# Attention scores in two six-bank units per half, where there were three four-bank units

## The chip, the cores and the metric

The kernel runs on one core of a Trainium2 chip. The metric is the device time of one execution in microseconds, lower is better. A core has five engines that run their own instruction streams and wait for each other by semaphores: TensorE (PE, with its weight loads as PEld), VectorE (DVE), ScalarE (ACT), GpSimd (POOL) and SyncE (SP). Matmul results land in PSUM, which has eight banks of 512 fp32 columns by 128 partitions.

## The reference, cut to what matters

```python
scores = scale * q @ k.T                     # 4 batches, 8 heads, 768 positions, head size 64
keep = (key < 8) | (0 <= query - key < 96)   # 8 global keys and a local window
scores = where(keep, scores - slope[h] * dist, -1e9)
a = softmax(scores); attn = a @ v
x = attn, heads side by side                 # 3072 tokens x 512
out = (relu(x @ w_gate) * (x @ w_val)) @ w_out   # 512 -> 1536 -> 512
```

Inputs and output are fp32. The kernel computes in bf16 and fp16 with fp32 accumulation.

## The kernel before, in words

**Tiling.** The work is cut into eight halves `s` = 0 to 7: half a sequence (384 queries) of one batch. A half with even `s` is a first half of its sequence, one with odd `s` a second half. For each half the kernel computes attention of eight heads, then the feed-forward part (FFN) of its 384 tokens. While the FFN of half `c` runs on TensorE, the attention of half `c + 1` is woven in between. The change is in the attention of `s` = 2 to 7 (the third to the eighth half); the first two go another way, which the change leaves alone.

**Attention of one half.** Heads come in pairs `p` = 0 to 3, a head of a pair is `e` = 0 or 1 and lies on rows 64·e to 64·e + 63 of the array. Two pairs make a double pair `pp`. Keys come in tiles `j`; a bank group `g` = 0, 1, 2 says which key tiles share one PSUM bank. For a fixed (`pp`, `g`, `e`) one bank holds the transposed scores of two heads. The steps are:

- `score_unit` (matmul at L512): it takes one bank for each (`pp`, `g`, `e`) of its unit and fills them. These matmuls use half of the array's rows, and the two of `e` = 0 and `e` = 1 stand one after the other, so that they can run side by side.
- `unit_exp` (L521): exp of one bank on ScalarE into a buffer `es` in SBUF. It gives back a function `mask`, which multiplies `es` by the precomputed mask and bias on VectorE (L533), one instruction per key tile of the bank.
- `piece_av` (L431): for one head, `es` times values and ones into a bank of `av_ps`, four matmuls in an even half and five in an odd one, in the order of the key tiles; then log of the sums on ScalarE (L440), and after the second head of a pair the reciprocal (L445).
- `piece_norm` (L450): two VectorE multiplications, from `av_ps` to `xT`, the FFN's input. They free the two `av_ps` banks.

In a list of pieces, X is one exp with, after it, the masks of the exp before it; X(unit) puts the score matmuls ahead of it. AV(p) is two pieces, one a head, and each first emits what masks are left (`flush`). N(p) is the normalisation, and `wait` is an empty slot.

**FFN of one half.** `gate(fc)` and `val(fc)` for `fc` = 0 to 11: four matmuls each (L745) into a bank of `ff_ps`; relu of the gate on ScalarE (L754); product with the value bank on VectorE into `ht` (L761). From `fc` = 7 on, one sum of `ht` tiles a step follows the product (L624 to L627, for `c` of 2 and more). Then the second product (L631) with pieces named "1", "2", "4", "6", "5", "7", "3", results added up on VectorE (L644), and stored.

**PSUM.** Three pools share the eight banks: `qk_ps` three, `av_ps` two, `ff_ps` three. A unit takes its banks from them.

**Order.** Everything is emitted in an order written out by hand. `weave` takes the FFN pieces, each with weight 0.65, and emits an attention piece whenever the emitted weight reaches its place; `spread` puts the n pieces of a half at equal distances over 85 or 87 per cent of it (for `s` = 2 between 2 and 86 per cent of its stretch). Each engine runs its instructions in the order of emission.

Of the kernel before, what the change touches and what calls it, by code (L numbers as in the profile page):

```python
# [8 lines left out]
FP32 = mybir.dt.float32  # L9
# [7 lines left out]
def kernel(  # L17
# [12 lines left out]
    nc = tc.nc  # L30
# [10 lines left out]
    NN = 3  # L41
# [45 lines left out]
    kT = [[const.tile([128, NT, 128], BF16, name=f"kT{i}_{p}") for p in range(HP)] for i in range(2)]  # L87
# [163 lines left out]
    QKB, FFB, AVB = (qk_psum, "qk_ps"), (ff_psum, "ff_ps"), (av_psum, "av_ps")  # L251
# [168 lines left out]
    def piece_av(s, p, e):  # L420
        b, half = divmod(s, 2)
        h = 2 * p + e
        vb = vbuf[b % 2]
        av = av_psum.tile([128, 512], FP32, name="av_ps")
        av_of[s, p, e] = av
        av3 = av[:, 0:QH].rearrange("d (n p) -> d n p", n=NN)
        todo = [t for bank in banks_of_half[half] for t in bank]
        for i, (j, a, w, m) in enumerate(todo):
            es, c = es_of[s, p, j, e]
            z0 = 2 * D * h + (D if e == 0 else 0)  # L430
            nc.tensor.matmul(av3[:, :, a : a + w],  # L431
                             lhsT=vb[:, j, z0 : z0 + 128],
                             rhs=es[:, c : c + NN * w].rearrange("k (n p) -> k n p", n=NN),
                             start=(i == 0), stop=(i == len(todo) - 1),
                             skip_group_check=True)
        o0, d0 = (0, 64) if e == 0 else (64, 0)
        if e == 0:
            av_of[s, p, "l"] = rc_pool.tile([128, QH], FP32, name="lnd")
        ln = av_of[s, p, "l"]
        nc.scalar.activation(ln[o0 : o0 + 64], av[d0 : d0 + 64, 0:QH], AF.Ln, bias=0.0, scale=1.0)  # L440
        if e == 1:
            if s not in xT_of:
                xT_of[s] = xt_pool.tile([128, N_DC, QH], BF16, name="xT")
            rc = rc_pool.tile([128, QH], FP32, name="rcp")
            nc.scalar.activation(rc, ln, AF.Exp, bias=0.0, scale=-1.0)  # L445
            av_of[s, p, "r"] = rc

    def piece_norm(s, p, e):
        r = slice(64 * e, 64 * e + 64)
        nc.vector.tensor_tensor(xT_of[s][r, p, :], av_of[s, p, e][r, 0:QH], av_of[s, p, "r"][r],  # L450
                                op=ALU.mult)

    def piece_av_wide(s, p, *pools):

        b, half = divmod(s, 2)
        todo = [t for bank in banks_of_half[half] for t in bank]
        pools = pools or (AVB,)
        av = [pool.tile([128, 512], FP32, name=name) for pool, name in (pools[0], pools[-1])]
        for what in range(2):
            av3 = av[what][:, 0:QH].rearrange("d (n p) -> d n p", n=NN)  # L460
            for i, (j, a, w, m) in enumerate(todo):
                for e in range(2):
                    es, ce = es_of[s, p, j, e]
                    z0 = D + 2 * D * (2 * p + e)
                    nc.tensor.matmul(av3[64 * e : 64 * e + 64, :, a : a + w],  # L465
                                     lhsT=ones if what == 0 else vbuf[b % 2][:, j, z0 : z0 + D],
                                     rhs=es[:, ce : ce + NN * w].rearrange("k (n p) -> k n p", n=NN),
                                     start=(i == 0), stop=(i == len(todo) - 1),
                                     skip_group_check=True)
        av_of[s, p] = av  # L470

    def piece_norm_wide(s, p):
        piece_sums_wide(s, p)
        piece_mul_wide(s, p)
# [17 lines left out]
            xT_of[s] = xt_pool.tile([128, N_DC, QH], BF16, name="xT")  # L492
        nc.vector.tensor_tensor(xT_of[s][:, p, :], av_of[s, p][1][:, 0:QH], av_of[s, p, "r"], op=ALU.mult)

    def score_unit(s, groups, pools):


        b, half = divmod(s, 2)
        out = []
        for pp, g in groups:  # L500
            banks = []
            for e in range(2):
                pool, name = pools.pop(0)
                banks.append(pool.tile([128, 512], FP32, name=name))
                out.append((pp, g, e, banks[e]))
            c = 0
            for j, a, w, m in banks_of_half[half][g]:
                for p in (2 * pp, 2 * pp + 1):
                    for e in range(2):
                        r = slice(64 * e, 64 * e + 64)  # L510
                        q3 = qT2[s % 2][r, p].rearrange("d (n p) -> d n p", n=NN)
                        nc.tensor.matmul(banks[e][:, c : c + NN * w], lhsT=kT[b % 2][p][r, j, :],  # L512
                                         rhs=q3[:, :, a : a + w], start=True, stop=True)
                    c += NN * w
        return out

    def unit_exp(s, pp, g, e, ps):
        bank = banks_of_half[s % 2][g]
        cols = sum(2 * NN * w for _, _, w, _ in bank)
        es = es_pool.tile([128, 480], BF16, name="es")  # L520
        nc.scalar.activation(es[:, 0:cols], ps[:, 0:cols], AF.Exp, bias=0.0, scale=scale)  # L521

        def mask():
            c = 0
            for j, a, w, m in bank:
                n_ = 2 * NN * w
                e4 = es[:, c : c + n_].rearrange("k (i n p) -> k i n p", i=2, n=NN)
                h0 = 4 * pp + e
                mk = m_all[:, h0 : h0 + 3 : 2, 0 if j == 0 else 1, :, m : m + w]
                if w == WQ:  # L530
                    e4 = e4.rearrange("k i n p -> k i (n p)")
                    mk = mk.rearrange("k i n p -> k i (n p)")
                nc.vector.tensor_mul(e4, e4, mk)  # L533
                for i in range(2):
                    es_of[s, 2 * pp + i, j, e] = (es, c + i * NN * w)
                c += n_

        return mask

    def attention_pieces(s):  # L540
        masks, units = [], []

        def flush():
            for f in masks:
                f()
            masks.clear()

        def scores(groups, pools):
            units.extend(score_unit(s, groups, list(pools)))

        def x(scored=None):
            ready = masks[:]
            masks.clear()
            if scored:
                scores(*scored)
            masks.append(unit_exp(s, *units.pop(0)))
            for f in ready:
                f()

        U = [([(0, 0), (0, 1)], (AVB, QKB, QKB, QKB)),  # L560
             ([(0, 2), (1, 0)], (AVB, QKB, QKB, QKB)),
             ([(1, 1), (1, 2)], (AVB, QKB, QKB, QKB))]
        X = lambda u=None: [(0.0, lambda: x(u))]
        AV = lambda p: [(0.0, lambda e=e: (flush(), piece_av(s, p, e))) for e in range(2)]
        N = lambda p: [(0.0, lambda: (piece_norm(s, p, 0), piece_norm(s, p, 1)))]
        wait = [(0.0, lambda: None)]
        a0, a1 = AV(0), AV(1)

        return (X(U[0]) + X() + X() + X() + wait + X(U[1]) + X() + X() + a0[0:1] + X() + a0[1:2] + N(0) + wait
                + X(U[2]) + X() + a1[0:1] + X() + X() + a1[1:2] + N(1) + wait * 2 + AV(2) + N(2) + wait * 2  # L570
                + AV(3) + N(3))


    out_v = out.rearrange("(s p n) d -> s n p d", p=128, n=NN)

# [261 lines left out]
    def AV(s, p, *pools):  # L837
        piece_av_wide(s, p, *pools)
        piece_norm_wide(s, p)
# [139 lines left out]
    def T2_piece(p):  # L979
# [10 lines left out]
    sums_wo = [(0.0, f) for i in (0, 3) for f in weight_sums(i, i + 3)]  # L990
    weave(f1_0[G[2]] + f1_1[G[2]] + f2_0 + f2_1,
          spread(attention_pieces(2), 0.02, 0.86), spread(early_pieces(3), 0.1, 0.76),
          spread(sums_wo, 0.08, 0.4))

    for c in range(2, NHALF):
        placed = []
        if c + 1 < NHALF:
            placed.append(spread(attention_pieces(c + 1), 0.0, 0.85 if c % 2 else 0.87))
        if c + 2 < NHALF:
            load_qk(c + 2, 0, H)  # L1000
            load_v_half(c + 2)
            placed.append(spread(early_pieces(c + 2), 0.25, 0.75))
        f1, f2 = ffn_pieces(c)
        weave(f1 + f2, *placed)
# [35 lines left out]
```

The softmax here doesn't subtract the row's maximum and nothing guards it: scores larger than these inputs give would overflow.

## Time and profile before

| what | value |
|---|---|
| median of 3 runs | 237.72 us (236.86 to 237.77) |
| span of the profiled execution | 236.1 us |
| PE busy | 228.7 us, 97% |
| DVE busy | 186.9 us, 79% |
| ACT busy | 146.2 us, 62% |
| POOL busy | 89.0 us, 38% |
| score matmuls, L512 | 216, in 18 units of 8, 12 or 16 |
| attention times values, L431 | 216 matmuls, 21.4 us |
| masks, L533 | 108 instructions, 29.9 us |

An engine's busy time is the sum of its instructions' times as recorded. Matmuls overlap in the pipeline, so that TensorE's pace is read from the distance of starts rather than from durations. The granted TensorE clock is full over nearly all of the span.

### The profile page before, as it was taken

The numbers are of one execution on the slowest core, as the hardware profiler recorded it, in microseconds if no ns is written. First come the engines' busy times: TensorE is split into PE (matmuls) and PEld (weight loads), VectorE is DVE, ScalarE is ACT, GpSimd is POOL, SyncE is SP. The second block draws the span as 40 slices with busy tenths as digits, with TensorE's granted clock in tenths as the row PEclk, the third lists the DMA queues.
The fourth block names the chain that finished last, engine by engine and source line by source line (L and its number), as shares of the span: only waits on it lengthen the run. The fifth ranks groups of instructions, "written<-read, shape, count | busy, mean of one in ns | idle before, by whom it ended". The sixth has DMA issues, their size and how long they took to land.

```text
span 236.1 us, 5512 instructions
## 1 busy us (share of the span) xinstructions
PE 228.7 (97%) x2021; PEld 157.7 (67%) x2021; DVE 186.9 (79%) x466; ACT 146.2 (62%) x321; POOL 89.0 (38%) x191
## 2 busy tenths in 40 slices
PE   7898999999999999999999999999999999999994
PEld 3674766656678666856688566856688566865683
DVE  6876867879988779886999779876899779863784
ACT  7988865667624887467842787557742687624310
POOL 8997913933483066406580066405340000000000
PEclk9999999999999999999999999999999999999999
DMA  5999999998459856856397764846412200020005
GB/s 167 203 168 183 206 262 282 171 118 267 72 155 170 250 149 106 52 176 204 90 81 119 236 175 90 53 143 214 93 44 89 92 0 3 0 92 0 1 3 178
DMA packets 71419, 30.43 MB, mean 129 GB/s; under 512 B 47744, under 2 KB 70784, under 8 KB 71392
## 3 DMA queue, kind: packets, MB, share of 16 engines
q0 software_dynamic: 34896, 10.27, 38.7%
q1 hardware_dynamic: 36496, 19.82, 29.7%
q8 instruction: 16, 0.26, 0.5%
q14 instruction: 11, 0.09, 0.1%
HBM read 28.38 MB, written 6.29 MB: 147 GB/s over the span
## 4 chain that ended last, share of the span: by engine, by line
PE 83%; DVE 5%; POOL 4%; DMA 4%; ACT 2%; issue 1%; POOLq 0%; DVEq 0%
PE ff_ps L745 49%; PE ff_ps L631 19%; PE av_ps L431 6%; DMA kc<-in_q_dram 4%; PE ff_ps L778 2%; PE av_ps L512 2%; PE qk_ps L512 2%; POOL vbuf L154 1%; DVE wo_sum L597 1%; DVE obuf L644 1%; DVE ht L761 1%; DVE es L533 1%; POOL kc L131 1%; PE av_ps L465 1%; POOL wg L171 1%
## 5 line engine op out<-in xcount | busy, mean ns | idle before, releaser
L754 ACT ACTIVATE grelu<-ff_ps 128x384 bf16<-128x384 f32 x96 | 46.8, 489 | 52.6 <-PE ff_ps L745 39.3
L745 PE MATMUL ff_ps<-xT,wg 128*128 128x384 bf16 x384 | 77.9, 326 | 0.2 <-DMA wg<-in_moe_w_gate_dram 0.2
L745 PE MATMUL ff_ps<-xT,wv 128*128 128x384 bf16 x384 | 77.9, 326 | 0.0
L761 DVE TENSOR_TENSOR ht<-ff_ps,grelu 128x384 f16<-128x384 f32 x96 | 53.4, 557 | 27.6 <-PE ff_ps L745 23.5
L745 PEld LDWEIGHTS <-wv 128*128 128x128 bf16 x384 | 36.0, 98 | 23.9 <-issue 1.1
L745 PEld LDWEIGHTS <-wg 128*128 128x128 bf16 x384 | 36.3, 97 | 21.7 <-issue 0.7
L450 DVE TENSOR_TENSOR xT<-av_ps,rcp 64x384 bf16<-64x384 f32 x48 | 26.6, 553 | 6.1 <-ACT rcp L445 5.3
L367 POOL CAST kc<-ks 128x384 bf16<-128x384 f32 x20 | 10.6, 569 | 54.5 <-DMA ks<-in_k_dram 54.5
L644 DVE TENSOR_TENSOR obuf<-ff_ps,obuf 128x512 f32<-128x512 f32 (+1 forms) x46 | 27.6, 604 | 3.6 <-PE ff_ps L631 0.9
L440 ACT ACTIVATE lnd<-av_ps 64x384 f32<-64x384 f32 x48 | 23.3, 485 | 11.1 <-PE av_ps L431 10.2
L533 DVE TENSOR_TENSOR es<-es,m_all 128x432 bf16<-128x432 bf16 (+3 forms) x108 | 29.9, 321 | 0.2 <-ACT es L521 0.2
L521 ACT ACTIVATE es<-qk_ps 128x432 bf16<-128x432 f32 (+2 forms) x54 | 27.6, 531 | 0.0
L154 POOL DMA_DIRECT2D vbuf<-in_v_dram x29 | 24.7, 860 | 0.1
L431 PEld LDWEIGHTS <-vbuf 128*128 128x128 bf16 x216 | 18.2, 98 | 4.8 <-DVE xT L450 0.4
L431 PE MATMUL av_ps<-es,vbuf 128*128 128x216 bf16 (+4 forms) x216 | 21.4, 226 | 0.0
L631 PEld LDWEIGHTS <-ht 128*128 128x128 f16 x198 | 18.6, 97 | 3.5 <-issue 0.8
L631 PEld LDWEIGHTS <-hsum 128*128 128x128 f16 x192 | 18.5, 98 | 2.1
L631 PE MATMUL ff_ps<-wo_sb,ht 128*128 128x256 f16 x132 | 18.3, 272 | 0.0
L631 PE MATMUL ff_ps<-wo_sum,hsum 128*128 128x256 f16 x144 | 17.2, 272 | 0.0
L445 ACT ACTIVATE rcp<-lnd 128x384 f32<-128x384 f32 x24 | 12.6, 523 | 0.8
L521 ACT ACTIVATE es<-av_ps 128x432 bf16<-128x432 f32 (+2 forms) x18 | 9.5, 527 | 2.0 <-PE qk_ps L512 2.0
L512 PEld LDWEIGHTS <-kT 64*128 64x128 bf16 x216 | 6.6, 94 | 6.1 <-issue 3.8
(130 smaller groups left out, 263.6 us busy)
## 6 DMA issues: line engine op xcount, KB each, us to landing
out_dram<-obuf SPq DMA_DIRECT2D x22, 256.0 KB
ks<-in_k_dram SPq DMA_DIRECT2D x5, 768.0 KB
qs<-in_q_dram SPq DMA_DIRECT2D x5, 768.0 KB
vbuf<-in_v_dram POOLq DMA_DIRECT2D x23, 120.0 KB, 4.7
wv<-in_moe_w_val_dram POOLq DMA_DIRECT2D x3, 512.0 KB, 10.5
wo_sb<-in_moe_w_out_dram POOLq DMA_DIRECT2D x1, 1536.0 KB, 21.0
wg<-in_moe_w_gate_dram POOLq DMA_DIRECT2D x2, 512.0 KB, 10.3
ks<-in_k_dram SPq DMA_DIRECT2D x4, 192.0 KB
```

The costliest lines, as they stand in the source:

```text
L154: nc.gpsimd.dma_start(out=v_dst(b, NG + r0, NG + r0 + n, j), in_=v[b, :, KT * j + r0 : KT * j + r0 + n, :].rearrange("h p d -> p h d"))
L431: nc.tensor.matmul(av3[:, :, a : a + w], lhsT=vb[:, j, z0 : z0 + 128], rhs=es[:, c : c + NN * w].rearrange("k (n p) -> k n p", n=NN), star ...
L440: nc.scalar.activation(ln[o0 : o0 + 64], av[d0 : d0 + 64, 0:QH], AF.Ln, bias=0.0, scale=1.0)
L450: nc.vector.tensor_tensor(xT_of[s][r, p, :], av_of[s, p, e][r, 0:QH], av_of[s, p, "r"][r], op=ALU.mult)
L512: nc.tensor.matmul(banks[e][:, c : c + NN * w], lhsT=kT[b % 2][p][r, j, :], rhs=q3[:, :, a : a + w], start=True, stop=True)
L521: nc.scalar.activation(es[:, 0:cols], ps[:, 0:cols], AF.Exp, bias=0.0, scale=scale)
L533: nc.vector.tensor_mul(e4, e4, mk)
L631: nc.tensor.matmul(ps[:, c0 : c0 + DH], lhsT=lhs(i), rhs=rhs(i), start=(i == 0), stop=(i == NP - 1), skip_group_check=True)
L644: add = lambda o, x, y: nc.vector.tensor_tensor(o, x, y, op=ALU.add)
L745: nc.tensor.matmul(st[key][:, 0:QH], lhsT=w_of(w, dc, fc), rhs=xT_of[c][:, dc, :], start=(dc == 0), stop=(dc == N_DC - 1))
L754: nc.scalar.activation(gr, psg[:, 0:QH], AF.Relu, bias=0.0, scale=1.0)
L761: nc.vector.tensor_tensor(ht[:, fc, :], psv[:, 0:QH], st["r", fc], op=ALU.mult)
```

## The change

A half's six groups of scores (two double pairs by three groups, each with two banks) were done in three units of two groups and four banks: one `av_ps` bank and the three `qk_ps` banks each time. The second unit mixed the two double pairs. Now each double pair is one unit of six banks: for `e` = 0 one `ff_ps` bank and both `av_ps` banks, for `e` = 1 the three `qk_ps` banks. So there are two units a half. The score matmuls, exps and masks are the same in number and size; their banks, their grouping and the order in a half differ. The list of pieces grows from 30 to 34 slots for the same stretch of FFN work. The exps now come `e` = 0 first, groups 0 to 2, then `e` = 1.

It is for fewer changes between full-array and half-row matmuls, and a simpler order.

```diff
-    def score_unit(s, groups, pools):
+    def score_unit(s, pp):
...
-        for pp, g in groups:
-            banks = []
-            for e in range(2):
-                pool, name = pools.pop(0)
-                banks.append(pool.tile([128, 512], FP32, name=name))
-                out.append((pp, g, e, banks[e]))
+        banks = {}
+        for e, pools in enumerate(((FFB, AVB, AVB), (QKB, QKB, QKB))):
+            for g, (pool, name) in enumerate(pools):
+                banks[e, g] = pool.tile([128, 512], FP32, name=name)
+        for g in range(3):
             c = 0
...
-        U = [([(0, 0), (0, 1)], (AVB, QKB, QKB, QKB)),
-             ([(0, 2), (1, 0)], (AVB, QKB, QKB, QKB)),
-             ([(1, 1), (1, 2)], (AVB, QKB, QKB, QKB))]
...
-        return (X(U[0]) + X() + X() + X() + wait + X(U[1]) + X() + X() + a0[0:1] + X() + a0[1:2] + N(0) + wait
-                + X(U[2]) + X() + a1[0:1] + X() + X() + a1[1:2] + N(1) + wait * 2 + AV(2) + N(2) + wait * 2
-                + AV(3) + N(3))
+        for pp in range(2):
+            out += X(pp) + X() * 2 + wait + X() * 3 + wait
+            for p in (2 * pp, 2 * pp + 1):
+                out += AV(p) + N(p) + wait * 2
+        return out[:-2]
```

More of the change, by code (lines that the diff above doesn't have):

```diff
@@ L493, in piece_mul_wide @@
         nc.vector.tensor_tensor(xT_of[s][:, p, :], av_of[s, p][1][:, 0:QH], av_of[s, p, "r"], op=ALU.mult)
-    def score_unit(s, groups, pools):
+    def score_unit(s, pp):
         b, half = divmod(s, 2)
-        out = []
-        for pp, g in groups:
-            banks = []
-            for e in range(2):
-                pool, name = pools.pop(0)
-                banks.append(pool.tile([128, 512], FP32, name=name))
-                out.append((pp, g, e, banks[e]))
+        banks = {}
[3 more added lines that the diff above has]
+        for g in range(3):
             c = 0
@@ L511, in score_unit @@
                         q3 = qT2[s % 2][r, p].rearrange("d (n p) -> d n p", n=NN)
-                        nc.tensor.matmul(banks[e][:, c : c + NN * w], lhsT=kT[b % 2][p][r, j, :],
+                        nc.tensor.matmul(banks[e, g][:, c : c + NN * w], lhsT=kT[b % 2][p][r, j, :],
                                          rhs=q3[:, :, a : a + w], start=True, stop=True)
                     c += NN * w
-        return out
+        return [(pp, g, e, ps) for (e, g), ps in banks.items()]
     def unit_exp(s, pp, g, e, ps):
@@ L546, in flush, with x @@
             masks.clear()
-        def scores(groups, pools):
-            units.extend(score_unit(s, groups, list(pools)))
-        def x(scored=None):
+        def x(pp=None):
             ready = masks[:]
             masks.clear()
-            if scored:
-                scores(*scored)
+            if pp is not None:
+                units.extend(score_unit(s, pp))
             masks.append(unit_exp(s, *units.pop(0)))
@@ L558, in x @@
                 f()
-        U = [([(0, 0), (0, 1)], (AVB, QKB, QKB, QKB)),
-             ([(0, 2), (1, 0)], (AVB, QKB, QKB, QKB)),
-             ([(1, 1), (1, 2)], (AVB, QKB, QKB, QKB))]
-        X = lambda u=None: [(0.0, lambda: x(u))]
+        X = lambda pp=None: [(0.0, lambda: x(pp))]
         AV = lambda p: [(0.0, lambda e=e: (flush(), piece_av(s, p, e))) for e in range(2)]
@@ L566, in attention_pieces @@
         wait = [(0.0, lambda: None)]
-        a0, a1 = AV(0), AV(1)
-        return (X(U[0]) + X() + X() + X() + wait + X(U[1]) + X() + X() + a0[0:1] + X() + a0[1:2] + N(0) + wait
-                + X(U[2]) + X() + a1[0:1] + X() + X() + a1[1:2] + N(1) + wait * 2 + AV(2) + N(2) + wait * 2
-                + AV(3) + N(3))
+        out = []
+        for pp in range(2):
[3 more added lines that the diff above has]
+        return out[:-2]
     out_v = out.rearrange("(s p n) d -> s n p d", p=128, n=NN)
```

## The prediction

> **What bounds the kernel now.** I read the page first (engines, then the chain of waits), then the timelines of TensorE and VectorE around the score units, then the waits of TensorE.
>
> ```profile
> PE 228.7 (97%) x2021; PEld 157.7 (67%) x2021; DVE 186.9 (79%) x466; ACT 146.2 (62%) x321; POOL 89.0 (38%) x191
> ...
> PE 83%; DVE 5%; POOL 4%; DMA 4%; ACT 2%; issue 1%; POOLq 0%; DVEq 0%
> ```
>
> The chain that ended last is TensorE for 83% of the span. The timeline shows that this is real streaming: from about 62 us on, FFN blocks of four matmuls follow each other at 0.65 us (four of 0.163 us, 384 columns each, so 0.42 ns a column). So a matmul pause removed is gained, and one added is lost. This is a score unit of half `s` = 4 on TensorE's timeline (start, length, engine, line, operation, tiles):
>
> ```profile
> 100.33 0.81 PE L745 MATMUL ff_ps<-xT,wg 128*128 128x384 bf16 x4
> 101.08 0.26 PE L512 MATMUL av_ps<-qT,kT 64*128 64x216 bf16 x1
> ...
> 101.55 0.82 PE L745 MATMUL ff_ps<-xT,wv 128*128 128x384 bf16 x4
> 102.21 0.81 PE L745 MATMUL ff_ps<-xT,wg 128*128 128x384 bf16 x4
> ```
>
> The block before it would hand over at 100.33 + 0.65 = 100.98; the next starts at 101.55. The unit costs 0.57 us. Its 8 matmuls run two at a time, four times 216 columns or 0.36 us of streaming. So 0.21 us is entry and exit. The other two units of this half, read the same way, cost 0.57 and 0.55 us. Together 1.69 us, for 1.0 us of streaming (2,400 columns after pairing): 0.23 us of overhead a unit.
>
> The second thing to see is VectorE. TensorE and VectorE in half `s` = 3, ahead of the AV piece of pair 2 at 92.58 us:
>
> ```profile
> 89.67 0.47 PE L431 MATMUL av_ps<-es,vbuf 128*128 128x72 bf16 x5
> 89.98 0.81 PE L745 MATMUL ff_ps<-xT,wv 128*128 128x384 bf16 x4
> ...
> 92.58 0.47 PE L431 MATMUL av_ps<-es,vbuf 128*128 128x72 bf16 x5
> ```
>
> ```profile
> 88.16 0.86 DVE L533 TENSOR_TENSOR es<-es,m_all 128x384 bf16<-128x384 bf16 x4
> 89.29 0.56 DVE L761 TENSOR_TENSOR ht<-ff_ps,grelu 128x384 f16<-128x384 f32 x1 [0.27 <-PE ff_ps L745]
> 89.89 0.42 DVE L624 TENSOR_TENSOR hsum<-ht 128x512 f16<-128x512 f16 x1
> 90.23 0.67 DVE L533 TENSOR_TENSOR es<-es,m_all 128x432 bf16<-128x432 bf16 x2
> 90.90 0.56 DVE L761 TENSOR_TENSOR ht<-ff_ps,grelu 128x384 f16<-128x384 f32 x1
> 91.37 0.41 DVE L625 TENSOR_TENSOR hsum<-hsum,ht 128x512 f16<-128x512 f16 x1
> 91.70 1.13 DVE L450 TENSOR_TENSOR xT<-av_ps,rcp 64x384 bf16<-64x384 f32 x2
> 92.87 0.56 DVE L761 TENSOR_TENSOR ht<-ff_ps,grelu 128x384 f16<-128x384 f32 x1
> ```
>
> From 89.29 on VectorE has no gap. Its costs from start to start are: a product 0.47 (90.90 to 91.37), or 0.60 where the sum behind it reads its result; a sum 0.33; the masks of a 432-column bank 0.33, of a 480-column bank 0.42 (half of the 0.86 for four). The last masks of the half end at 90.90, 1.7 us before the AV piece of pair 2. That slack keeps VectorE off the path now.
>
> **What the Trainium skill says.** "TensorEngine Tiling (Array Packing)", section Key Properties, says that a change of the tiling mode drains TensorE. Score matmuls are 64 rows, all around them 128; the 0.23 us a unit agrees. "PSUM — Partial Sum Buffer", section Engine vs sequencer instructions, says that VectorE's and ScalarE's queues are strictly first in, first out, and that matmuls start in program order. So a mask waits behind every product emitted ahead of it, and the whole FFN waits behind an AV matmul that lacks one mask. The timelines agree in that no row overtakes another.
>
> **The change part by part.**
>
> *Units.* Matmuls and columns are the same, 18 units become 12. Six times 0.23 is 1.4 us off TensorE's path.
>
> *Feed-forward bank.* The unit's first matmuls need an `ff_ps` bank. By the banks given out in the new order it is the one of the gate a block or two earlier, whose relu starts 0.85 us after its block (relus follow their gates at this distance on ScalarE) and takes 0.49. I find it done just before the unit in all halves, by 0.06 to 0.4 us; the next two blocks likewise. Cost 0, no better than close.
>
> *Both attention banks.* The second unit needs both freed by N(1). From the end of an AV pair to the first multiplication's end takes 1.66 us, to the second's 2.25 us where nothing interferes (log 0.51, reciprocal 0.51, 0.58 each). In odd halves three FFN blocks (1.96 us) lie between, plus entry and the first groups of the unit (0.1 and 0.2 or 0.4 us): 0.05 to 0.4 us to spare. In even halves there are four blocks. Cost 0.
>
> *Order, odd halves (`s` = 3, 5, 7).* I placed the 34 pieces by the spread's formula, 0.516 of weight apart. From the second unit U on it gives, with g and v for gate and val, A20 and A21 for the two heads of pair 2 (A30 further down is the first of pair 3):
>
> ```
> after:  g7 U v7 X g8 X v8 X g9 X v9 X g10 v10 A20 A21 g11 N2 v11
> before: g6 U v6 X A10 g7 X v7 X g8 A11 v8 N1 g9 v9 g10 A20 v10 A21 g11 N2
> ```
>
> The masks of an X come with the next X, those of the last with A20. A21 needs the last masks (`e` = 1, `g` = 2) for its fifth matmul. TensorE gets there 7 blocks of 0.65, A20's 0.31 and four matmuls (0.24) after v7 starts: 5.10 us. VectorE starts v7's product 0.92 us after that (as the trace has it for a val block) and must then do four products with the `ht` sums that begin at `fc` = 7 (4 x 0.47 + 0.12 + 4 x 0.34 = 3.4 us) and six banks of masks (4 x 0.42 + 2 x 0.33 = 2.3 us): end at 6.6 us. TensorE stalls for about 1.55 us, and behind A21 stands all of the FFN. Before, four of these exps were left after the last unit, and A20 and A21 came one block later after them. Three halves: +4.6 us.
>
> *Order, even halves (`s` = 4, 6).* A20 falls behind piece "2" and A21 behind "4"; the masks end about when A21 asks, cost 0.1. But N(2) now comes after piece "6", so it stands on VectorE behind that piece's addition and a sum, where before it stood ahead of them:
>
> ```profile
> 121.01 0.55 DVE L624 TENSOR_TENSOR qT<-ht 128x768 f16<-128x768 f16 x1
> 121.83 1.14 DVE L450 TENSOR_TENSOR xT<-av_ps,rcp 64x384 bf16<-64x384 f32 x2 [0.27 <-ACT rcp L445]
> 123.00 0.69 DVE L644 TENSOR_TENSOR obuf<-ff_ps,obuf 128x512 f32<-128x512 f32 x1
> 123.61 0.55 DVE L625 TENSOR_TENSOR qT<-qT,ht 128x768 f16<-128x768 f16 x1
> ```
>
> Counted from A21's end: "6" takes 0.65, its addition starts at 0.87, lasts 0.61, the sum 0.46, the first multiplication ends at 2.5. A30 asks at 1.96 (18 matmuls). Stall 0.55. Two halves at 0.65: +1.3 us.
>
> *Half `s` = 2.* Here sums of `w_out` fill VectorE too. The last masks of the first unit end at about 55.3 us on the old clock, A01's third matmul asks at 54.6: +0.7 us. In return this old wait goes (total us, times, longest):
>
> ```profile
> PE av_ps L512 <- DVE xT L450: 0.2, 1, 0.2
> ```
>
> and a similar pause of some 0.15 us at an AV piece of `s` = 5 (145 us). Together -0.35.
>
> *Sum.* -1.4 + 4.6 + 1.3 + 0.7 - 0.35 = +4.85 us, so 237.7 + 4.9 = 242.6 us.
>
> **The bounds of what is unknown.** The row times above are from quiet stretches. In the groups by shape the means of the masks lie up to 0.05 us higher (the 432-column one 0.40, where quiet ones take 0.37), since some are stretched while GpSimd copies (one took 0.68 us at 57.35). With minimum values an odd half's stall is 1.3 us, with mean ones 1.7 us. The close waits could each slip by 0.1 to 0.3 us a half.
>
> **The rivals.**
>
> 1. *The forecast*: VectorE's queue in front of A21 sets three stalls of 1.3 to 1.7 us, the order of N(2) two of half a microsecond; 240.5 to 244.5 us. For it: VectorE has no gap after 89.29 us even now. Chance 0.57.
> 2. *Faster*: only the drains count and the masks come in time. 237.7 - 1.4 - 0.35 = about 236 us. It would need VectorE's work in front of A21 to take 4.2 us rather than 5.7. Against it are the row times; for it, that TensorE's 97% makes every drain count. Chance 0.10.
> 3. *Given back*: stalls of about 0.3 us a half at A21 and at the close waits eat the 1.4 us. Near 237.7 us. Chance 0.08.
> 4. *Half of it*: the odd stalls are about 0.8 us, since VectorE gets ahead somewhere or an earlier pause lets it catch up. 237.7 - 1.75 + 2.4 + 1.3 + 0.5 = about 240.2 us. Chance 0.10.
> 5. *Worse*: the close waits on banks fail as well, some 0.5 us a half, and the masks take their mean values. 242.6 + 3 + 0.6 = about 246 us. For it: margins of 0.1 us and less. Chance 0.15.
>
> **How the numbers follow.** The predicted time is that of the first case. The range from 239.3 to 245.7 us reaches through the fourth case into the fifth and leaves out the second, the third and the far part of the fifth. Faster by over 0.5% (below 236.5) is the second case, 0.10; within 0.5% the third, 0.08; slower the rest, 0.82.
>
> **What would show it.** Right: score units of 16 and 20 matmuls at about 0.73 and 0.83 us from block to block; TensorE idle before L431, released by VectorE's masks, over 1 us three times, in odd halves at pair 2; idle before A30 of even halves, released by `xT`. The steps on banks are wrong if TensorE waits ahead of score units or ahead of the FFN block after them. The forecast as a whole is wrong if the AV pieces of pair 2 start without a gap; then the VectorE sum above was too long, and the time is under 237 us.

## The result and the profile after

| | median us | range us | ratio to before, 95% interval |
|---|---|---|---|
| before | 237.68 (6 runs) | 236.86 to 237.77 | 1 |
| after | 245.96 (6 runs) | 245.00 to 247.56 | 1.0362 [1.0323, 1.0400] |

The change makes the kernel 8.3 us slower. The prediction had the direction, but 4.85 us as the size; the time lies 0.3 us above the range.

The engines and the chain on the page of after, and the line of the AV matmuls (attention times values, L431), first of before, then of after, with the line of after's masks:

```profile
PE 229.1 (94%) x2021; PEld 158.8 (65%) x2021; DVE 186.8 (77%) x466; ACT 145.5 (60%) x321; POOL 90.7 (37%) x191
...
PE 21%; DVE 2%; ACT 1%; issue 1%; DVEq 0%
...
L431 PE MATMUL av_ps<-es,vbuf 128*128 128x216 bf16 (+4 forms) x216 | 21.4, 226 | 0.0
L431 PE MATMUL av_ps<-es,vbuf 128*128 128x216 bf16 (+4 forms) x216 | 22.6, 226 | 5.9 <-DVE es L531 4.9
L531 DVE TENSOR_TENSOR es<-es,m_all 128x432 bf16<-128x432 bf16 (+5 forms) x108 | 29.9, 322 | 0.3 <-ACT es L519 0.2
```

No engine's busy time has grown by more than 2 us; TensorE's share fell from 97 to 94% because the span grew. The chain now covers only the last quarter of the span, so it can't be used as it was before. (Busy time counts a stretch in which matmuls overlap once; it is not the sum of their durations.) What is new stands in the AV line: TensorE stood idle for 5.9 us ahead of AV matmuls, where it was 0.0 before, and 4.9 of it was ended by VectorE's masks (L531). TensorE's waits show the same by releaser (total us, times, longest):

```profile
PE av_ps L431 <- DVE es L531: 4.9, 8, 1.1
...
PE av_ps L431 <- DVE xT L450: 0.9, 2, 0.5
...
PE ff_ps L738 <- DVE ht L754: 0.5, 1, 0.5
```

Recorded idle understates such a stop, since the ends of the matmuls before it are modelled. I therefore measure a stop by starts: from the start of a piece to the start of the next block, less the time that it takes where nothing waits (0.65 us for an FFN block, 0.305 for an AV piece of an odd half, 0.26 of an even one).

**Score units.** TensorE's timeline after, a unit of `s` = 4:

```profile
102.86 0.81 PE L738 MATMUL ff_ps<-xT,wg 128*128 128x384 bf16 x4
103.61 0.26 PE L510 MATMUL ff_ps<-qT,kT 64*128 64x216 bf16 x1
...
104.25 0.82 PE L738 MATMUL ff_ps<-xT,wv 128*128 128x384 bf16 x4
```

104.25 - 102.86 - 0.65 = 0.74 us for 16 matmuls, as predicted (0.73), and no idle is recorded ahead of a unit. From block to block the 12 units of after cost 9.30 us together. The 18 of before cost 10.95 us, 0.20 of it the old wait of half `s` = 2; the units themselves save 1.45 us.

**The worst place.** VectorE in half `s` = 5 of after:

```profile
146.91 1.58 DVE L531 TENSOR_TENSOR es<-es,m_all 128x144 bf16<-128x144 bf16 x4
148.41 0.55 DVE L754 TENSOR_TENSOR ht<-ff_ps,grelu 128x384 f16<-128x384 f32 x1
148.88 0.62 DVE L618 TENSOR_TENSOR hsum<-hsum,ht 128x512 f16<-128x512 f16 x1
149.42 1.14 DVE L531 TENSOR_TENSOR es<-es,m_all 128x432 bf16<-128x432 bf16 x3
...
152.46 0.37 DVE L531 TENSOR_TENSOR es<-es,m_all 128x432 bf16<-128x432 bf16 x1
```

TensorE beside it:

```profile
147.65 0.81 PE L738 MATMUL ff_ps<-xT,wv 128*128 128x384 bf16 x4
149.01 0.81 PE L738 MATMUL ff_ps<-xT,wg 128*128 128x384 bf16 x4 [0.54 <-DVE ht L754]
...
150.30 0.57 PE L431 MATMUL av_ps<-es,vbuf 128*128 128x72 bf16 x7
151.68 0.30 PE L431 MATMUL av_ps<-es,vbuf 128*128 128x192 bf16 x2 [0.80 <-DVE es L531]
152.89 0.27 PE L431 MATMUL av_ps<-es,vbuf 128*128 128x216 bf16 x1 [0.91 <-DVE es L531]
153.00 0.81 PE L738 MATMUL ff_ps<-xT,wg 128*128 128x384 bf16 x4
```

The ten AV matmuls from 150.30 are A20 and A21. The fifth of A21 starts at 152.89, just after the mask of 152.46 ends. From 150.30 to 153.00 are 2.70 us, less 0.61: A21 stopped TensorE for 2.09 us. Earlier, the gate block at 149.01 lost 149.01 - 147.65 - 0.65 = 0.71 us: it needs a bank that a late product frees. Four masks took 1.58 us here; the same four take 0.86 in `s` = 3, where GpSimd is quiet. GpSimd's timeline shows its key reordering at that time:

```profile
146.85 0.54 POOL L278 COPY kT<-kN 128x360 bf16<-128x360 bf16 x1 [3.31 <-DVE ht L754]
...
147.76 0.66 POOL L278 COPY kT<-kN 128x360 bf16<-128x360 bf16 x1
...
148.68 0.53 POOL L278 COPY kT<-kN 128x360 bf16<-128x360 bf16 x1
```

**The account.** The stops by starts, against the terms predicted:

| term | predicted us | trace of after, us |
|---|---|---|
| score units, 12 for 18 | -1.4 | -1.45 |
| banks | 0 | 0 |
| A21 of `s` = 3, 5, 7 | +4.6 | 1.67 + 2.09 + 1.48 = +5.24 |
| gate block of `s` = 5 | none | +0.7 |
| A21 of `s` = 4, 6 | +0.2 | 0.31 + 0.39 = +0.70 |
| A30 of `s` = 4, 6 | +1.1 | 0.61 + 0.61 = +1.22 |
| A01 of `s` = 2 | +0.7 | +0.78 |
| old waits | -0.35 | about -0.1 |
| sum | +4.85 | about +7.1 |

The profiled spans differ by 7.4 us (243.5 against 236.1); about 0.5 of this stands already at the first score unit (48.83 us against 48.31), ahead of everything changed. The last 0.9 us to the 8.3 of the medians is not in this one execution; the runs on GpSimd and the section on the hardware come back to it.

### The profile page after: what moved, and what is told of

Read it like the earlier page. It is cut to its first block, busy times and chain, and to the rows that moved or that the text cites. A ratio compares the mean times of both kernels' runs of the same rounds, so it can differ in the third digit from the quotient of the medians.

```text
span 243.5 us, 5517 instructions
## 1 busy us (share of the span) xinstructions
PE 229.1 (94%) x2021; PEld 158.8 (65%) x2021; DVE 186.8 (77%) x466; ACT 145.5 (60%) x321; POOL 90.7 (37%) x191
## 5 line engine op out<-in xcount | busy, mean ns | idle before, releaser
L367 POOL CAST kc<-ks 128x384 bf16<-128x384 f32 x20 | 9.6, 527 | 58.4 <-DMA ks<-in_k_dram 58.4
L531 DVE TENSOR_TENSOR es<-es,m_all 128x432 bf16<-128x432 bf16 (+5 forms) x108 | 29.9, 322 | 0.3 <-ACT es L519 0.2
L431 PE MATMUL av_ps<-es,vbuf 128*128 128x216 bf16 (+4 forms) x216 | 22.6, 226 | 5.9 <-DVE es L531 4.9
L431 PEld LDWEIGHTS <-vbuf 128*128 128x128 bf16 x216 | 18.2, 98 | 11.8 <-issue 4.2
L624 PE MATMUL ff_ps<-wo_sb,ht 128*128 128x256 f16 x132 | 17.8, 272 | 0.0
L519 ACT ACTIVATE es<-qk_ps 128x432 bf16<-128x432 f32 (+2 forms) x36 | 17.6, 533 | 0.0
L519 ACT ACTIVATE es<-av_ps 128x432 bf16<-128x432 f32 (+2 forms) x24 | 11.9, 525 | 0.0
L367 POOL CAST qc<-qs 128x384 bf16<-128x384 f32 x20 | 9.9, 538 | 1.0 <-DMA qs<-in_q_dram 1.0
```

The source lines that it names most:

```text
L367: nc.gpsimd.tensor_copy(dst[s % 2].rearrange("t n (h d) -> t h n d", d=D)[:, 2 * p : 2 * p + 2], src[s][:, 2 * p : 2 * p + 2, :].rearrange ...
L431: nc.tensor.matmul(av3[:, :, a : a + w], lhsT=vb[:, j, z0 : z0 + 128], rhs=es[:, c : c + NN * w].rearrange("k (n p) -> k n p", n=NN), star ...
L624: nc.tensor.matmul(ps[:, c0 : c0 + DH], lhsT=lhs(i), rhs=rhs(i), start=(i == 0), stop=(i == NP - 1), skip_group_check=True)
```

## The experiments

The ratio is always to runs of before on the same chip; before's median was 237.5 to 237.7 us each time.

**Are the terms of the sum right?** First, a drain alone: before, with each score unit of two groups split into two units.

```diff
+        H = [((g[0:1], pools[0:2]), (g[1:2], pools[2:4])) for g, pools in U]
-        return (X(U[0]) + X() + X() + X() + wait + X(U[1]) + X() + X() ...
+        return (X(H[0][0]) + X(H[0][1]) + X() + X() + wait + X(H[1][0]) + X(H[1][1]) + X() ...
```

> The kernel before, with each score unit cut into its two groups, the second put one X later, so that a half has six entries into half-row matmuls in place of three; same matmuls, exps, masks, banks. Term of the drains: 18 more units of 0.23 us, +4.1 us, about 241.8 us. If the entry and exit of a unit cost nothing on the path (the gain in my sum was no gain), within 0.5 us of before.

Measured: 240.97 us, 1.0143 [1.0109, 1.0178]; +3.3 us for 18 more units is 0.18 us each (0.14 to 0.24 by the interval). The score matmuls now come as two islands (102.77 is the second):

```profile
102.01 0.82 PE L746 MATMUL ff_ps<-xT,wv 128*128 128x384 bf16 x4
102.77 0.36 PE L512 MATMUL qk_ps<-qT,kT 64*128 64x216 bf16 x4
103.06 0.34 PE L746 MATMUL ff_ps<-xT,wg 128*128 128x384 bf16 x1
```

So 12 units for 18 save 1.1 to 1.5 us. The gain that the change is for is real.

Second, a feed-forward bank in a unit, in the order of before: `FFB` in place of `AVB` in all three units.

```diff
-        U = [([(0, 0), (0, 1)], (AVB, QKB, QKB, QKB)),
+        U = [([(0, 0), (0, 1)], (FFB, QKB, QKB, QKB)),
...
```

> The kernel before, its three units kept, but the first bank of each from the feed-forward pool in place of the attention pool. Theory of VectorE's queue: the bank is no cost, within 0.5 us of 237.7 us. Rival, the feed-forward part starves while a unit holds one of its three banks: some 0.3 to 0.5 us a unit, 18 units, 5 us or more slower.

Measured: 239.26 us, 1.0063 [1.0039, 1.0086]: +1.5 us, where no cost was expected. One part is a wait of half `s` = 2. From block to block that unit takes 1.49 us, where the old wait made it 0.77:

```profile
PE ff_ps L778 <- DVE ht L761: 0.9, 1, 0.9
```

The other part is spread out: in ten of the other 17 units the FFN block behind the unit waits for the relu that frees its bank, for 0.12 to 0.19 us each. The first unit of `s` = 4 is one of them:

```profile
100.99 0.81 PE L745 MATMUL ff_ps<-xT,wg 128*128 128x384 bf16 x4
...
102.38 0.81 PE L745 MATMUL ff_ps<-xT,wv 128*128 128x384 bf16 x4
```

102.38 - 100.99 - 0.65 = 0.74 us, for 0.57 in before. All ten come out at 0.74 us. (By starts the two parts are 2.2 us; the profiled execution of this run reaches its first unit 0.5 us sooner than before's.) A bank taken from the FFN is thus not free for a short unit; the units of after take 0.74 to 0.81 us, and no block behind one waits there. And 1.5 us with 18 such units can't be the 8.3.

**Is it the last masks?** After, without the masks of the second head of the pairs of double pair 1: 27 of the 108 mask instructions (the expectation counted 30), among them those that A21 waits for. The heads concerned are computed unmasked.

```diff
-                nc.vector.tensor_mul(e4, e4, mk)
+                if (pp, e) != (1, 1):
+                    nc.vector.tensor_mul(e4, e4, mk)
```

> The changed kernel without the multiplications by the mask for the second double pair's heads with e = 1, three banks a half, so those heads' weights stay unmasked and 30 VectorE instructions of about 0.25 us fall away. Everything else stays in its place. VectorE's queue as the cause: the waits at pair 2's second head go, some 1.6 + 2.8 + 1.5 us in odd halves and 0.7 us in even ones, less 1 us that may reappear further on: 239 to 241.5 us. If VectorE's masks are not what TensorE waits for, no change from 246 us.

Measured: 239.25 us, 1.0077 [1.0062, 1.0092], which is 6.7 us less than after. In its trace the stops at A21 of the odd halves are gone, those at A30 of the even ones are not:

```profile
PE av_ps L431 <- DVE xT L450: 0.9, 2, 0.5
```

So most of what the change costs hangs on VectorE's masks, as TensorE waits for them at A21. This doesn't tell whether the masks come late because of their place in the queue or because they take longer; the next four do.

**Its place in the queue.** After, with the sums of `ht` tiles taken out from between the products and done later:

```diff
-            if c > 1 and 7 <= fc < N_FC - 1:
-                if fc == 7:
-                    first[0] = pair.sums(0, 4)
-                first[0][fc - 7]()
...
-        late = pair.sums(0 if c < 2 else 4, NP)
+        late = pair.sums(0, NP)
```

> The changed kernel, with the four sums of ht tiles that stand between products and masks from the eighth block on moved behind the products, into the pieces of the second matmul, in one go over all six tiles. Theory of VectorE's queue: 4 x 0.34 us fewer in front of the last mask, so each odd half waits 1.3 us less; 4 us at most, less what the longer late sums give back in piece 6 (0 to 0.5 us a half): 242 to 244.5 us. Rival, the bank: no change from 246 us.

Measured: 244.47 us, 1.0274 [1.0248, 1.0299]. The odd stops at A21 fell from 1.5 to 2.1 us to 0.68 to 0.72. In the even halves A21 rose from 0.3 to 0.4 us to 1.0, as the later sums now stand ahead of their last masks; and the second product waits for the sums. So four sums of 0.34 us in the queue are about 1 us of stop in each odd half, but moving them gives most of it back elsewhere.

After, with the AV pieces of pair 2 two FFN blocks later in odd halves:

```diff
+    def moved(placed, n, moves):
+        return [(at + moves.get(i, 0.0) / n, f) for i, (at, f) in enumerate(placed)]
...
-            placed.append(spread(attention_pieces(c + 1), 0.0, 0.85 if c % 2 else 0.87))
+            placed.append(moved(spread(attention_pieces(c + 1), 0.0, 0.85 if c % 2 else 0.87),
+                                38 if c % 2 else 31, {} if c % 2 else {26: 2.0, 27: 2.0, 28: 2.0, 31: 1.9, 32: 1.2, 33: 1.0}))
```

> The changed kernel, with the attention times values of pair 2 in odd halves two feed-forward blocks later (and what follows it moved along). Theory of VectorE's queue: TensorE's wait for the masks in each odd half falls by up to the 1.3 us that the two blocks take, three halves, so 3.5 to 4 us faster than the changed kernel, about 242.2 us. Rival, the bank: no change from 246 us, since units and banks stay where they are.

Measured: 244.31 us, 1.0276 [1.0226, 1.0325], not the 242.2 expected. Its waits:

```profile
PE av_ps L431 <- DVE es L531: 2.3, 5, 0.6
PE ff_ps L738 <- DVE ht L754: 1.3, 4, 0.5
```

A21's stop fell only to 0.7 us. The expectation left out that the last masks are emitted with A20, so that they moved back too, behind one more product. VectorE in `s` = 7:

```profile
207.43 0.56 DVE L754 TENSOR_TENSOR ht<-ff_ps,grelu 128x384 f16<-128x384 f32 x1
207.91 0.37 DVE L531 TENSOR_TENSOR es<-es,m_all 128x432 bf16<-128x432 bf16 x1
```

Two blocks less one product are 1.30 - 0.47 = 0.83 us, and the stop of this half fell from 1.48 to 0.66 us. In `s` = 3 and 5 four FFN blocks now wait for banks that late products free, 1.9 us by starts. There GpSimd copies beside the masks (four masks took 1.21 and 1.24 us); in `s` = 7, where it doesn't (0.86 us), one block waits, for 0.17 us. So a later A21 takes its masks along, and where VectorE is held up, part of the stop comes back at FFN blocks.

**GpSimd beside the masks.** The prediction's sum held the masks at their quiet times; stretched ones were in its range alone. A first attempt placed GpSimd's key reordering later in the order of emission:

```diff
-            placed.append(spread(early_pieces(c + 2), 0.25, 0.75))
+            early = spread(early_pieces(c + 2), 0.25, 0.75)
+            placed.append(early[:-HP] + spread(early[-HP:], 0.8, 1.0))
```

> The changed kernel with GpSimd's reordering of keys for the half after the next moved from 65 to 74 per cent of a half, where the masks of the second unit are, to 80 to 100 per cent. If GpSimd's copies stretch VectorE's masks (1.1 us of it in half 5 of the profiled run), 1 to 2 us faster than the changed kernel, 244 to 245 us, and less spread between runs. If the stretching has another source, no change from 246 us.

Measured: 245.17 us, 1.0335 [1.0306, 1.0363], within the interval of after. It doesn't answer the question: every engine, GpSimd too, has its instructions in the same order as in after. So it serves as a second measurement of after, and its trace shows what the first didn't. In `s` = 3 GpSimd's copies begin at 91.33 us, where they began at 93.12 in after, and so they meet masks in this half too (VectorE's lines behind GpSimd's):

```profile
91.33 0.68 POOL L278 COPY kT<-kN 128x360 bf16<-128x360 bf16 x1 [2.99 <-DMA kN<-kc]
...
90.88 1.19 DVE L531 TENSOR_TENSOR es<-es,m_all 128x144 bf16<-128x144 bf16 x4
...
93.01 1.14 DVE L531 TENSOR_TENSOR es<-es,m_all 128x432 bf16<-128x432 bf16 x3
```

The same masks took 0.86 and 0.77 us in after. A21 of `s` = 3 stops for 2.32 us here, for 1.67 there, and a gate block ahead of it for 0.33. GpSimd's work for that half waits for the loading of keys, which came 1.8 us sooner in this execution (its first cast starts at 84.35 us, for 86.15). How many halves are hit thus changes from one execution to the next, with the order of instructions unchanged.

The second attempt leaves the key reordering out from the fifth half on; scores there use an earlier batch's keys, so that TensorE, VectorE and ScalarE have the same instructions in the same order, on other data.

```diff
-            placed.append(spread(early_pieces(c + 2), 0.25, 0.75))
+            placed.append(spread(early_pieces(c + 2), 0.25, 0.75)[:-HP])
```

> The changed kernel without GpSimd's reordering of the transposed keys from the fifth half on (the scores then use keys that an earlier batch left). No other engine's instructions change. If GpSimd's copies are what stretches VectorE's masks, the waits at pair 2 fall to 1.5 us in each of the three odd halves and no clock window is lost: 243.5 to 244.5 us, with a spread below 1 us. If not, 246 us and the same stretched masks.

Measured: 243.63 us, 1.0253 [1.0226, 1.0280]; 2.3 us below after, 1.5 below the run before this one. VectorE in `s` = 5, the same instructions as above:

```profile
147.34 0.85 DVE L531 TENSOR_TENSOR es<-es,m_all 128x144 bf16<-128x144 bf16 x4
148.12 0.55 DVE L754 TENSOR_TENSOR ht<-ff_ps,grelu 128x384 f16<-128x384 f32 x1
148.59 0.41 DVE L618 TENSOR_TENSOR hsum<-hsum,ht 128x512 f16<-128x512 f16 x1
148.92 0.76 DVE L531 TENSOR_TENSOR es<-es,m_all 128x432 bf16<-128x432 bf16 x3
```

and TensorE:

```profile
150.04 0.57 PE L431 MATMUL av_ps<-es,vbuf 128*128 128x72 bf16 x7
150.80 0.30 PE L431 MATMUL av_ps<-es,vbuf 128*128 128x192 bf16 x2 [0.19 <-DVE es L531]
152.02 0.27 PE L431 MATMUL av_ps<-es,vbuf 128*128 128x216 bf16 x1 [0.92 <-DVE es L531]
152.12 0.81 PE L738 MATMUL ff_ps<-xT,wg 128*128 128x384 bf16 x4
```

The four masks take 0.85 us, not 1.58, the next three 0.76, not 1.14. VectorE's busy time fell from 186.8 to 184.7 us with the same 466 instructions. The gate block no longer waits. From A20 to the next gate are 2.08 us, less 0.61: 1.47 us, and the two other odd halves have 1.48, where the prediction had 1.55. A21 of the even halves stops for 0.05 and 0.19 us (predicted 0.1), A30 for 0.61 (predicted 0.55). With GpSimd out of the way the prediction's two queue steps come out to 0.1 us.

**The order of N(2).** After, with N(2) of even halves directly behind A21:

```diff
-            placed.append(spread(attention_pieces(c + 1), 0.0, 0.85 if c % 2 else 0.87))
+            placed.append(moved(spread(attention_pieces(c + 1), 0.0, 0.85 if c % 2 else 0.87),
+                                38 if c % 2 else 31, {28: -0.9} if c % 2 else {}))
```

> The changed kernel with pair 2's normalisation in even halves emitted right behind its second head, ahead of the addition of piece 6. If the order on VectorE makes TensorE's wait at pair 3 (0.61 us, twice), 1.2 us faster than the changed kernel, about 244.8 us. If the wait is for ScalarE's log and reciprocal, no change.

Measured: 246.00 us, 1.0333 [1.0288, 1.0378]. In the trace both stops of 0.61 us at A30 are gone, for 0.2 us more ahead of a piece of the second product; so the mechanism of this step holds. The median doesn't show the gain: three of its four runs (245.85 to 246.38 us) had a mean TensorE clock of 0.993, and the one at 0.999 took 243.99. The section on the hardware comes back to that. In the profiled execution, one of the three, the copies met the masks of `s` = 3 as well (A21 stops for 2.17 us).

**A version that keeps the gain.** Three runs put the mendings together. The first has the early sums over two of the six pairs of `ht` tiles, not four, at `fc` = 3 to 6, not 7 to 10; pieces of pairs 2 and 3 moved back in odd halves; N(2) forward in even ones; and two pieces moved in half 2. (It also has the first attempt's placing of the key reordering, which again changed no order.)

```diff
-            if c > 1 and 7 <= fc < N_FC - 1:
+            if c > 1 and 3 <= fc < 7:
...
-        late = pair.sums(0 if c < 2 else 4, NP)
+        late = pair.sums(0 if c < 2 else 2, NP)
...
+                                38 if c % 2 else 31, {28: -0.9} if c % 2 else {27: 1.0, 28: 1.0, 31: 1.0, 32: 1.0, 33: 1.0}))
```

> Two units with the order mended: a third of the ht sums at the fourth to seventh block, the rest in the second matmul's pieces; GpSimd's key order late; pair 2's second head one block later in odd halves; its normalisation early in even ones; pair 0's second head one block later in half 2. If VectorE's order is all that costs, the waits fall from 9.5 us to about 2 us and the drains' 1.2 us are gained: 237 to 239 us. If the bank or something else is part of it, 240 us or more.

Measured: 238.90 us, 1.0053 [1.0033, 1.0072]. The stops left add up to 4.1 us, 1.2 of them in half 2. The second moved more of the even halves' pieces, and half 2 from its piece 9 on one block later:

```diff
-          spread(attention_pieces(2), 0.02, 0.86), spread(early_pieces(3), 0.1, 0.76),
-          spread(sums_wo, 0.08, 0.4))
+          moved(spread(attention_pieces(2), 0.02, 0.86), 38, dict.fromkeys(range(9, 34), 1.0)), spread(early_pieces(3), 0.1, 0.76),
+          spread(sums_wo, 0.22, 0.56))
```

> Two units with the order mended further than in the mix before: in half 2 everything from the first attention head on one block later and the sums of the output weights later; in even halves pair 2's first head one block earlier, so that the last masks stand ahead of half of the ht sums, and pair 3 one block later; in odd halves pair 3 later. The waits should fall from 4.1 us to 1.5 us or less: 235.8 to 237.2 us, up to 0.7% faster than the kernel before. If two units cost something apart from VectorE's order, 238 us or more.

Measured: 239.10 us, 1.0064 [1.0041, 1.0086]: a miss. The other halves fell to 1.6 us of stops, but half 2 rose to 2.9, as its last masks now ran into the sums of `w_out`:

```profile
PE av_ps L431 <- DVE es L531: 1.3, 2, 1.0
```

The third therefore leaves half 2 in three units of four banks as before and has two units of six in `s` = 3 to 7, 13 units in all, with the same early sums:

```diff
+            placed.append(moved(spread(attention_pieces6(c + 1), 0.0, 0.85 if c % 2 else 0.87),
+                                38 if c % 2 else 31, {26: -1.0, 27: 1.0, 28: 0.1, 31: 1.0, 32: 1.0, 33: 1.0} if c % 2 else {27: 1.0, 28: 1.0, 31: 1.9, 32: 1.2, 33: 1.0}))
```

> Three units of four banks in half 2, as before the change; two units of six banks in halves 3 to 7, with the mended order: early ht sums, pair 2's heads apart and its normalisation right behind them, pair 3 later. Ten entries into half-row matmuls where five times three were, 5 fewer by 0.19 to 0.25 us, and waits of about 1.5 us against 1.1 us before: 236.3 to 237.0 us. If two units cost something apart from VectorE's order, 238 us or more.

And the control, before with the early sums alone:

```diff
-            if c > 1 and 7 <= fc < N_FC - 1:
+            if c > 1 and 3 <= fc < 7:
...
-        late = pair.sums(0 if c < 2 else 4, NP)
+        late = pair.sums(0 if c < 2 else 2, NP)
```

> The kernel before with the early ht sums alone, as a control: its units and order stay. Its waits on VectorE are few, so no gain over 0.3 us, 237.2 to 238 us. If the gain of the mended two-unit kernel came from the sums and not from the units, this one would show the same gain.

Measured: 236.55 us over 13 runs, 0.9953 [0.9937, 0.9970], for the third; 238.33 us over 21 runs, 1.0033 [1.0019, 1.0046], for the control, 0.7 us slower than before, where no change was expected. So the third version beats before by 1.1 us and after by 9.4, and the early sums alone don't give that. Its chain is again TensorE's:

```profile
PE 83%; DVE 7%; POOL 3%; DMA 3%; ACT 2%; issue 1%; POOLq 0%; DVEq 0%; ACTq 0%
```

Five units fewer at 0.19 to 0.23 us are worth 1.0 to 1.2 us, as much as the whole gain. What still waits for masks is an AV piece in each of `s` = 3 and 5, 0.3 us each. That the units are the gain is this sum; its order was mended too, and no run had that order with the old units.

## Why the prediction was right in direction and wrong in size

- **Units, -1.4.** Right: -1.45 in the trace; the split of before's units gives 6 x 0.18, about 1.1 us.
- **Banks, 0.** Right in after: no score unit waits, nor an FFN block behind one. The feed-forward bank was close, as said: the ten units that wait for it in before's order take 0.74 us, and so do after's units of 16 matmuls. In before's order it costs 1.5 us.
- **Odd halves, three stops of 1.55.** The mechanism was right: VectorE's queue of products, sums and masks in front of A21's fifth matmul. Without GpSimd's key reordering the stops are 1.47 to 1.48 us. The term was mis-sized with it: 5.24 + 0.7 us in place of 4.6.
- **Even halves, 0.1 and 0.55.** Right without GpSimd's copies (0.05, 0.19 and 0.61). With them A21 stops for 0.31 and 0.39.
- **Half 2, +0.7 - 0.35.** The stop at A01 came (0.78). The gain of 0.35 did not: of two old waits one of 0.17 us went, the other stayed, 0.30 for 0.22.
- **The step that failed** is the size of the odd halves' term, and with it "The bounds of what is unknown". It let the masks be stretched by the mean excess of 0.05 us, which made an odd half's stop 1.7 us at most, 5.1 us for three; the trace of after has 5.9 us. That excess is an average over masks that mostly meet a quiet GpSimd. The masks' total didn't even grow: 29.9 us for 108 in both kernels. What changed is the place. In `s` = 5 of after four masks lose 0.7 us to the copies, a sum 0.2 and three masks 0.4, together 1.3 us; so the gate block and A21 stop for 0.7 and 0.6 us more than without the copies. A mean over quiet and disturbed instructions is no bound for a place in which all are disturbed. The trace of before had a sign of it: beside the first copy of `s` = 5 two masks took 1.01 us, and the same two in `s` = 3, which the prediction shows, 0.67 (VectorE's line behind GpSimd's):

```profile
143.81 0.72 POOL L278 COPY kT<-kN 128x360 bf16<-128x360 bf16 x1 [3.40 <-DVE ht L761]
...
143.75 1.01 DVE L533 TENSOR_TENSOR es<-es,m_all 128x432 bf16<-128x432 bf16 x2
```

- **The rival "worse" (246 us)** names the number measured, but not the cause: it needed failed waits at the units' banks, some 0.5 us a half, and these didn't come.

What stays open: without GpSimd's reordering the kernel is still 6.1 us above before (243.63 - 237.51), where the prediction had 4.85. Half 2 accounts for some 0.6 of this 1.25. The rest is not assigned to a place; the part ahead of everything changed differs by as much or more between the profiles (the first score unit starts at 48.31 us in before, 48.83 in after and 49.45 here).

## What to carry to other kernels

Fewer and larger units save a fixed cost each, but they also delay the last of their outputs; count, on the strictly ordered engine that finishes them, everything that is emitted ahead of that last one, up to the instruction that needs it. Where that engine has no gap, a later consumer or a shifted sum moves part of the stop elsewhere, so the whole stretch has to be balanced, and a half with other work beside it may be better left alone. Price an instruction at the place where it will stand, beside the engine that will run there, and not by its mean.

## What the runs showed of the hardware

**VectorE beside GpSimd.** The Trainium skill, "SBUF — State Buffer", section "SBUF: two separate sides", says that VectorE and GpSimd share a pair of ports as an exclusive lock, which concerns VectorE's operations with two SBUF inputs when a GpSimd operation reads SBUF; the later one is blocked for the whole instruction of the other. The traces agree in which instructions are stretched; they don't show the lock itself. Four masks (two SBUF inputs) took 1.58 us beside copies and 0.85 without, a sum of `ht` tiles 0.62 and 0.41, while the product, which reads a PSUM bank, took 0.55 both times. The size is about 1.3 us in one half, and 2.3 us in the kernel when the copies go, which includes what follows from the longer pauses.

**A pause can cost clock.** The same skill, "TensorE: Matmul & The Clock Gate", section "What's actually happening", says that TensorE's clock falls to half after an idle window of about 3.4 us, and that these windows run freely. This case differs: there was no whole idle window, and yet in the trace of the run with N(2) moved the clock falls to half behind two waits of 0.85 and 0.91 us (stretch in us; its length; busy us of PE, PEld, DVE, ACT and POOL with instructions; clock; DMA share; GB/s):

```profile
93.00:96.50 3.50, 1.73 (x16) 1.04 (x15) 3.35 (x10) 1.00 (x3) 3.50 (x9) 1.00 0.55 42
96.50:98.00 1.50, 1.50 (x10) 0.84 (x10) 0.23 (x1) 1.26 (x3) 1.08 (x2) 0.86 1.25 79
98.00:100.00 2.00, 2.00 (x13) 1.59 (x12) 1.87 (x5) 0.49 (x2) 0.00 (x0) 0.50 1.41 89
100.00:101.50 1.50, 1.50 (x14) 1.16 (x13) 0.56 (x3) 0.51 (x2) 0.00 (x0) 0.67 0.00 0
101.50:104.00 2.50, 2.50 (x25) 2.25 (x23) 1.39 (x3) 0.98 (x2) 0.00 (x0) 1.00 0.00 0
```

TensorE was busy for 1.73 of the 3.5 us ahead; then the clock record is at half from 97.59 to 101.0 us. Two of after's six runs (246.63 and 247.56 us) had the same mean clock of 0.993, which is what one such window makes of the whole: 0.5 x 3.4 of 244 us; the other four, at 0.999 and above, took 245.00 to 246.05, on average 245.5. No run of before, of the best version, or of the kernel without key reordering had it, nor had the four of the first attempt, which have after's order. So a part of the excess over the profiled 7.4 us is probably such windows; only the mean clock of those two runs is known. Without them the median would be 245.6 us, and the copies' meeting with `s` = 3 may be some of the rest. That the pause sets the window off is inferred from their order in time; no run varied the pause alone.
